# A fused attention-and-MoE kernel: TensorE work in a hand-written order, one MoE wave around each attention group, phi(q) on eight 32x64 tiles, and the denominator inverted once per token

## The chip, the cores and the metric

The kernel runs on one core of one Trainium2 chip. The metric is device time in microseconds (us), the median of several executions. A run more than 1.5% above the fastest of the same kernel is called slow, and ratios use fast runs alone.

Names: PE is TensorE, PEld its weight loads, DVE VectorE, ACT ScalarE, POOL GpSimd, SP the queue that issues most DMAs. PSUM is the memory that TensorE writes. "L220" in a profile line is line 220 of that kernel's text, so one product has different line numbers in different kernels.

## The reference

```python
# q, k, v: (4 batches, 4 heads, 1088 tokens, 32); S1, S2: (8, 32)
def phi(x):                                   # 64 features
    a, b = S1 @ x, S2 @ x                     # 8 each, per token
    return outer(a, b).reshape(64)
kv  = sum over tokens of phi(k) v^T           # 64 x 32 per head
z   = sum over tokens of phi(k)
num = phi(q) @ kv
den = phi(q) @ z + 1e-6
x   = (num / den), heads side by side         # 4352 tokens x 128
h   = x @ w_in                                # 128 -> 2048
g   = h * sigmoid(beta * h)
out = g @ w_out                               # 2048 -> 128
```

All inputs and the output are f32. The attention part is computed in f32, the two large products of the MoE in f16.

## The kernel before

x is kept turned (128 features on partitions, tokens along the row). beta is folded into the weights, so that g becomes a plain Silu. The MoE is cut into chunks of 512 tokens. A *wave* is two of the sixteen 128-wide slices of d_ff for one chunk: two products into two PSUM banks, one Silu of 128x1024 on ACT, then two products into the output bank (68 waves in all).

```python
    def wave():
        # ... (cut)
        for jj in range(jn):
            nc.tensor.matmul(out=wv[:, jj * tw : (jj + 1) * tw],
                             lhsT=winp[:, (j0 + jj) * P : (j0 + jj + 1) * P],
                             rhs=xT[:, t0 : t0 + tw], start=True, stop=True)
        nc.scalar.activation(out=g, in_=wv, func=ACTF.Silu)
        flush_w2()                            # second products of the wave before
        # ... (cut)
```

Attention of a batch is a generator of steps; behind each step up to two waves are emitted, if their tokens are ready. The framework's scheduler then orders each engine. phi(q) has two heads in one block-diagonal weight of 128 columns, on the 64 rows of these heads:

```python
        for c0, cw in q_chk:                  # 384, 384, 320 tokens
            for pi in range(2):
                rows = slice(64 * pi, 64 * pi + 64)
                nc.tensor.matmul(out=aps[:, :cw], lhsT=sa[rows, :],
                                 rhs=qT[rows, c0 : c0 + cw], start=True, stop=True)
                nc.scalar.copy(out=asb[pi][:, :cw], in_=aps[:, :cw])
            # ... (cut: bps with sb in the same way, then qp = bps * asb on DVE)
```

The denominator comes out of its product repeated for the 32 features of each head, and the whole of it is inverted:

```python
            for which, dst in ((1, den), (0, num)):
                for pi in range(2):
                    nc.tensor.matmul(out=dst[64 * pi : 64 * pi + 64, :cw],
                                     lhsT=nd[:, which, 64 * pi : 64 * pi + 64],
                                     rhs=qp[:, pi, c0 : c0 + cw], start=True, stop=True)
            nc.scalar.activation(out=deps[:, :cw], in_=den[:, :cw], func=ACTF.Identity, bias=epsb)
            nc.vector.reciprocal(out=deps[:, :cw], in_=deps[:, :cw])       # 128 x 384
            nc.vector.tensor_tensor(out=xT[:, ...], in0=num[:, :cw], in1=deps[:, :cw], op=MUL)

    for b in range(B):
        steps = attention(b)
        # ... (cut: weights prepared in batch 0)
        for _ in steps:
            pump(2)                           # two waves behind each step
    pump(10**6)
```

## Time and profile before

| what | value | view |
|---|---|---|
| time | 181.4 us | median of 3 runs |
| span | 180.2 us | page |
| busy PE, ACT, DVE | 82%, 49%, 45% | page, part 1 |
| first MoE wave | 41.1 us | timeline |
| period of a batch (den to den) | 37.1, 37.7, 34.7 us | chain of waits |
| tail, two waves | 2.19 us | timeline of ACT |

Two lines of the page of the kernel before: PE's busy time with its count of instructions, and the TensorE clock that was granted, in tenths, in 40 equal slices of the span.

```profile
PE 147.1 (82%) x1201; PEld 59.9 (33%) x1201; DVE 82.0 (45%) x113; ACT 88.9 (49%) x122; POOL 15.0 (8%) x17
...
PEclk9999999699999999969999999999999995799998
```

PE is the bound, but the MoE streams only 2 x 69,632 columns, and in the chain two matmuls of 512 take 0.43 us, so it needs about 58 us of the 147. The rest is attention, switching and slow clock. The chain of waits of the kernel before, inside a batch (start, length, what):

```profile
85.86 0.43 PE wave L220 x2
86.29 0.84 PE aps L293 x2
87.13 0.54 PE moeout L180 x2
87.67 0.43 PE wave L220 x2
...
90.34 0.85 PE bps L301 x4
91.19 0.54 PE wave L220 x2
```

A lone aps product (two records, as every f32 product here) takes 0.84 us; two bps products on the two row halves take 0.85 together. A pair of MoE matmuls takes 0.43, and 0.54 when it follows an attention group. Next the groups of instructions of the kernel before: line, engine, operation, out<-in, shapes, count, busy us, mean ns.

```profile
L359 DVE RECIPROCAL deps<-deps 128x384 f32<-128x384 f32 (+1 forms) x12 | 28.4, 2395 | 7.0 <-ACT deps L358 7.0
...
L293 PE MATMUL aps<-qT,sa 64*128 64x384 f32 (+1 forms) x48 | 22.0, 581 | 0.1
...
L301 PE MATMUL bps<-qT,sb 64*128 64x384 f32 (+1 forms) x48 | 16.5, 544 | 0.0
```

And the end of attention in a batch, from the timeline of the kernel before (start, length, engine, what; in brackets the idle time before it and what ended it):

```profile
71.24 4.96 DVE L359 RECIPROCAL deps<-deps 128x384 f32<-128x384 f32 x2 [1.98 <-ACT deps L358]
...
76.12 0.96 DVE L360 TENSOR_TENSOR xT<-num,deps 128x384 f16<-128x384 f32 x2
...
76.67 1.33 PE L350 MATMUL num<-qp,nd 128*64 128x320 f32 x2 [3.15 <-DVE xT L360]
77.94 1.89 PE L220 MATMUL wave<-xT,winp 128*128 128x512 f16 x4
```

DVE inverts for 5 us, PE stands for 3.15, and then four wave matmuls take 1.89 us instead of 0.87: the clock has been halved (the 6 in slice 18 of the clock row; 0.58 granted in the mean from 76 to 80 us).

### The profile page before, as it was taken

To read this page: it belongs to the slowest core of one execution; us is meant where nothing else is said; L and a number is where in the kernel's file an instruction comes from. 1 tells how busy PE (TensorE), PEld (TensorE's weight loads), DVE (VectorE), ACT (ScalarE), POOL (GpSimd) and SP (SyncE) were. 2 spreads that over 40 slices of the span, in tenths; PEclk is the share of its full clock that TensorE was granted. 3 is DMA by queue.
4 is the path that set the end of the run, shared out by engine and by line. 5 is a ranking of instruction groups with operands and counts; after the bars stand their busy time and mean duration, and the time that the engine had idled before them with its cause. 6 is when DMAs were issued, how large, how long until landed. Compare 5 with 4: busy or idle time off the path is not lost.

```text
span 180.2 us, 2944 instructions
## 1 busy us (share of the span) xinstructions
PE 147.1 (82%) x1201; PEld 59.9 (33%) x1201; DVE 82.0 (45%) x113; ACT 88.9 (49%) x122; POOL 15.0 (8%) x17
## 2 busy tenths in 40 slices
PE   0079996849999998399999977999999738988870
PEld 0023555312333363023333632333336202333350
DVE  1268374798725322977032128954222496101010
ACT  0230132119666745054966452869664215588870
POOL 2006340000320000000500000005000000000000
PEclk9999999699999999969999999999999995799998
DMA  5699999300003000030003000300300300002131
GB/s 182 169 382 340 318 249 254 93 4 2 0 0 58 5 4 0 0 58 0 0 7 55 4 0 0 58 4 0 58 0 4 52 6 4 0 0 41 19 60 29
DMA packets 22480, 11.35 MB, mean 63 GB/s; under 512 B 18738, under 2 KB 20802, under 8 KB 22338
## 3 DMA queue, kind: packets, MB, share of 16 engines
q1 hardware_dynamic: 22304, 11.15, 25.1%
q8 instruction: 9, 0.15, 0.3%
q10 hardware_dynamic: 162, 0.02, 0.1%
q14 instruction: 5, 0.03, 0.1%
HBM read 8.94 MB, written 2.23 MB: 62 GB/s over the span
## 4 chain that ended last, share of the span: by engine, by line
PE 68%; ACT 9%; DVE 9%; issue 7%; DMA 4%; ACTq 0%; SPq 0%; DVEq 0%
PE wave L220 17%; PE moeout L180 16%; PE aps L293 10%; ACT g L228 7%; PE kvz L314 6%; PE bps L301 5%; PE kps L261 5%; DVE deps L359 4%; PE bb L152 4%; PE num L350 3%; DMA v<-in_v_dram 3%; PE den L350 2%; DMA sraw<-in_S_dram 1%; ACT deps L358 1%; DVE xT L360 1%
## 5 line engine op out<-in xcount | busy, mean ns | idle before, releaser
L228 ACT ACTIVATE g<-wave 128x1024 f16<-128x1024 f32 x68 | 66.2, 1021 | 28.9 <-PE wave L220 28.7
L220 PE MATMUL wave<-xT,winp 128*128 128x512 f16 (+1 forms) x144 | 42.7, 387 | 5.0 <-DVE xT L360 4.4
L180 PE MATMUL moeout<-g,woutp 128*128 128x512 f16 (+1 forms) x144 | 41.9, 375 | 4.0 <-ACT g L228 4.0
L359 DVE RECIPROCAL deps<-deps 128x384 f32<-128x384 f32 (+1 forms) x12 | 28.4, 2395 | 7.0 <-ACT deps L358 7.0
L304 DVE TENSOR_TENSOR qp<-bps,asb 128x384 f32<-128x384 f32 (+1 forms) x24 | 12.4, 533 | 30.2 <-PE bps L301 30.0
L293 PE MATMUL aps<-qT,sa 64*128 64x384 f32 (+1 forms) x48 | 22.0, 581 | 0.1
L220 PEld LDWEIGHTS <-winp 128*128 128x128 f16 x144 | 13.2, 100 | 26.2 <-issue 15.5
L180 PEld LDWEIGHTS <-woutp 128*128 128x128 f16 x144 | 12.1, 98 | 26.7 <-issue 17.7
L297 ACT COPY asb<-aps 128x384 f32<-128x384 f32 (+1 forms) x24 | 11.2, 465 | 17.6 <-PE aps L293 12.8
L358 ACT ACTIVATE deps<-den,epsb 128x384 f32<-128x384 f32 (+1 forms) x12 | 6.7, 562 | 25.2 <-DVE xT L360 13.8
L277 POOL TENSOR_TENSOR kp<-kab 128x576 f32<-128x576 f32 x8 | 10.2, 1291 | 105.8 <-DVE kab L268 105.8
L350 PE MATMUL num<-qp,nd 128*64 128x384 f32 (+1 forms) x48 | 13.8, 535 | 5.7 <-DVE xT L360 5.7
L261 PE MATMUL kps<-kT,sw 32*32 32x288 f32 x128 | 9.4, 480 | 10.2 <-DVE sw L119 9.6
L301 PE MATMUL bps<-qT,sb 64*128 64x384 f32 (+1 forms) x48 | 16.5, 544 | 0.0
L190 DVE STREAM_TRANSPOSE o_sb<-moeout 128x512 f32<-128x512 f32 (+1 forms) x9 | 6.1, 676 | 19.1 <-PE moeout L180 19.0
L350 PE MATMUL den<-qp,nd 128*64 128x384 f32 (+1 forms) x48 | 10.7, 525 | 1.3 <-DVE nd L343 1.2
L293 PEld LDWEIGHTS aps<-qT,sa 64*128 64x128 f32 x48 | 7.9, 205 | 9.9 <-issue 8.0
L268 DVE STREAM_TRANSPOSE kab<-kps 128x288 f32<-128x288 f32 x16 | 7.2, 466 | 7.1 <-PE kps L261 7.1
L314 PE MATMUL kvz<-kp,ones 128*32 128x64 f32 (+1 forms) x288 | 9.5, 219 | 0.0
L314 PE MATMUL kvz<-kp,v 128*32 128x64 f32 (+1 forms) x288 | 9.3, 222 | 0.0
L301 PEld LDWEIGHTS bps<-qT,sb 64*128 64x128 f32 x48 | 7.4, 205 | 3.9 <-issue 1.3
L350 PEld LDWEIGHTS num<-qp,nd 128*64 128x64 f32 x48 | 4.2, 153 | 13.2 <-DVE xT L360 6.8
(43 smaller groups left out, 75.1 us busy)
## 6 DMA issues: line engine op xcount, KB each, us to landing
v<-in_v_dram SPq DMA_DIRECT2D x16, 144.0 KB, 8.4
k<-in_k_dram SPq DMA_DIRECT2D x4, 544.0 KB, 4.6
q<-in_q_dram SPq DMA_DIRECT2D x4, 544.0 KB
out_dram<-o_sb SPq DMA_DIRECT2D x20, 64.0 KB, 2.0
w_in_sb<-in_moe_w_in_dram SPq DMA_DIRECT2D x1, 1024.0 KB
out_dram<-o_sb SPq DMA_DIRECT2D x4, 56.0 KB, 1.9
out_dram<-o_sb SPq DMA_DIRECT2D x4, 48.0 KB
out_dram<-o_sb SPq DMA_DIRECT2D x4, 40.0 KB, 1.7
```

What stands on the lines that cost most here:

```text
L180: nc.tensor.matmul(out=moe["acc"][:, :tw], lhsT=woutp[:, j, :], rhs=g[:, jj, :tw], start=(j == 0), stop=(j == NJ - 1),)
L220: nc.tensor.matmul(out=wv[:, jj * tw : (jj + 1) * tw], lhsT=winp[:, (j0 + jj) * P : (j0 + jj + 1) * P], rhs=xT[:, t0 : t0 + tw], start=Tru ...
L228: nc.scalar.activation(out=g, in_=wv, func=ACTF.Silu)
L261: nc.tensor.matmul(out=kps[32 * g : 32 * g + 32, : NJK * 32], lhsT=sw[rows, :], rhs=kT[rows, KBASE[g] * 32 : (KBASE[g] + NJK) * 32], start ...
L277: eng.tensor_tensor(out=kp[:, h].rearrange("p j (i l) -> p j i l", i=R), in0=bass.AP(tensor=a0.tensor, offset=a0.offset, ap=[pst, [32, NJK ...
L293: nc.tensor.matmul(out=aps[:, :cw], lhsT=sa[rows, :], rhs=qT[rows, c0 : c0 + cw], start=True, stop=True)
L297: nc.scalar.copy(out=asb[pi][:, :cw], in_=aps[:, :cw])
L301: nc.tensor.matmul(out=bps[:, :cw], lhsT=sb[rows, :], rhs=qT[rows, c0 : c0 + cw], start=True, stop=True)
L304: nc.vector.tensor_tensor(out=qp[:, pi, c0 : c0 + cw], in0=bps[:, :cw], in1=asb[pi][:, :cw], op=MUL)
L314: nc.tensor.matmul(out=kvz[32 * h : 32 * h + 32, F * which : F * which + F], lhsT=v_t[b][:kr, h, j, :] if which == 0 else ones[:kr, :], rh ...
L350: nc.tensor.matmul(out=dst[64 * pi : 64 * pi + 64, :cw], lhsT=nd[:, which, 64 * pi : 64 * pi + 64], rhs=qp[:, pi, c0 : c0 + cw], start=Tru ...
L359: nc.vector.reciprocal(out=deps[:, :cw], in_=deps[:, :cw])
```

## The change

The intent: shorten what attention costs TensorE, shorten the way from den to x, and lay attention groups and waves in a fixed alternation so that ACT and PE always have work. Five parts:

1. **Order.** Each batch is 15 groups; a slot emits the first products of a wave, one group, then the second products of the wave before. TensorE's instructions are taken in the order of the text (`manual_schedule`).
2. **phi(q) on 32x64 tiles:** one head's 32 rows, 64 features, for one half of the tokens; up to eight such products at once. Token blocks of 32 alternate between the two halves of the partitions. num goes to 64x32 tiles, kps to 64x32.
3. **Denominator turned:** den has two useful rows per head (one for each half). DVE transposes 32x32 blocks, adds epsilon, inverts 18 columns, and transposes a broadcast of it back.
4. **Start:** two small loads of S1 and S2 instead of eight, q of batch 0 on ACT's queue, half of the broadcast of beta before anything else, the weights scaled on POOL.
5. PSUM is redivided: a product's PSUM tile has one or two banks, and `aps` shares the two buffers of the waves.

```diff
+    ctx.enter_context(tc.manual_schedule(engines={mybir.EngineType.PE}))
 ...
+    def slot(group=None):
+        if moe["ci"] < len(tok_chk) and sum(tok_chk[moe["ci"]]) <= moe["ready"]:
+            w1()
+        if group is not None:
+            group()
+        ...
+        while len(todo) > 1:
+            w2(*todo.pop(0))
 ...
+                for c in range(2):
+                    for m in range(2):
+                        for pr, n, dst, sx in mm:          # aps of one pair of heads, bps of the other
+                            h = 2 * pr + m
+                            rows = slice(32 * h, 32 * h + 32)
+                            nc.tensor.matmul(
+                                out=dst[64 * c : 64 * c + 64, m, : 32 * tn],
+                                lhsT=sx[rows, :],
+                                rhs=qT[rows, t0 : t0 + tn, c, :], ...)
 ...
-            nc.scalar.activation(out=deps[:, :cw], in_=den[:, :cw], func=ACTF.Identity, bias=epsb)
-            nc.vector.reciprocal(out=deps[:, :cw], in_=deps[:, :cw])
+                nc.vector.transpose(out=dT[...], in_=dps[:, :w])
+                nc.vector.tensor_scalar_add(rc[:, :tn], dT[:, :tn, :2], 1e-6)
+                nc.vector.reciprocal(out=rc[:, :tn], in_=rc[:, :tn])
+                nc.vector.transpose(out=rb[...], in_=<rc, each value 32 times>)
 ...
+        return [kps, ab((0, 0), None), ab((1, 0), (0, 0)), kv([1, 2]), ab((0, 1), (1, 0)),
+                kv([3, 4]), ab((1, 1), (0, 1)), kv([5, 6]), ab(None, (1, 1)), kv([7, 8, 0]),
+                ndt, den(0), num(0), den(1), num(1)]
 ...
-        for _ in steps:
-            pump(2)
+        for n, grp in enumerate(groups):
+            slot(grp)
+        slot()
+        slot()
```

## The prediction

> **What bounds the kernel now.** The span is 180.2 us. The page's first part has PE busy 82%, ACT 49%, DVE 45%; the chain of waits gives PE 68%, so TensorE is the bound, but much of it is not streaming. The two MoE products stream 2 x 69,632 columns; in the chain two back-to-back 512-column matmuls take 0.43 us, so the MoE needs about 58. Four things are lost around that (timeline, windows, chain):
>
> 1. Before the first MoE wave, at 41.1 us, only attention of batch 0 runs: sketch weights wait for eight small loads until 9.6, the broadcast of beta takes 7.2, the denominator section holds 32.7 to 41.1.
> 2. phi(q) (aps, bps): 22.0 and 16.5 us busy. A lone 64x128 product of 384 columns takes 0.84 us; two fit the array.
> 3. Every switch between MoE and attention products costs: a MoE pair takes 0.54 instead of 0.43 after one, and a group's last product drains about 0.2. The scheduler switches per product.
> 4. Denominator: reciprocal on 128x384 takes 2.53 us; all twelve, 28.4 us DVE. From den to the first xT a batch takes 5 to 7 us with PE mostly waiting, and the clock falls: 0.76 granted in 142 to 156, where four wave matmuls take 1.86 instead of 0.87.
>
> One batch's period (den to den) is 37.1, 37.7, 34.7 us.
>
> **What the change does.** The Trainium skill ("TensorEngine Tiling (Array Packing)", Available Configurations) lists 32x64 as eight tiles. The trace agrees that such small tiles run together: 11 kps products of 288 columns end within 0.74 us. So a full phi(q) group (four aps, four bps products, 288 or 256 columns) should take 0.6 to 0.7, five groups a batch 3.3, against about 7 now. den and num fall from 3.6 to about 2.2, kps to one group of 0.65. kvz keeps 2.2 but is cut in four groups (+0.8). Attention becomes about 10 us of PE per batch, MoE with one switch per slot 15.5.
> The reciprocal handles 18 columns (about 0.25, as rbeta's 16), plus two DVE transposes (288: 0.47; 576: about 0.75) and an add: 1.7 per chunk instead of 2.6 + ACT. ACT per batch: 16 waves x 1.08 + 4 asb copies x 0.65 + 0.4 = 20; DVE about 15. Neither binds overall, but in phi(q) slots ACT (1.02 + 0.65) matches PE (1.75).
>
> **Sum.** A slot with wave and group: 1.75 us. Per batch: 14 such, one num slot without a wave and with a bubble waiting for DVE (2.0), two wave-only slots bound by ACT (1.1 each): 28.7.
> Start: sketch weights earlier, half the beta broadcast before k lands, weights prepared on POOL; first wave near 27. Rest of batch 0: 5.5. Three batches: 86. Tail, 16 waves at the 1.095 of now: 17.5. Last product, transpose, output DMA: 5.5; launch 1.2. Sum 142.7; I add 3 for in-order stalls. **Predicted 146 us, range 138 to 158; faster 0.97, same 0.02, slower 0.01.**
>
> **What would show it.** First wave at 25 to 30 us. Period 27 to 31. aps+bps PE under half. DVE total under 75. Granted clock near 1.00 from the first wave on. Chain: PE and ACT, with DVE only at num. Tail rate unchanged.
>
> **What would make it wrong.** PE in hand order stops at any late operand: qT or kp late behind other DVE/POOL work, the single "two" bank pair, or aps sharing buffers with the waves (copy and Silu in one loop), giving 2.1 us slots and 158. Eight tiles not overlapping would add about 2 us per batch. Weights late from POOL would move the first wave past 30.

## The result

The changed kernel takes 142.9 us (141.7 to 143.7, 4 runs) against 181.6 us. The ratio is 0.786, with a 95% interval of 0.779 to 0.793. Ratios here are the mean time of one kernel's fast runs over that of the other's fast runs of the same rounds, so they are not quite the ratio of the medians.

The same lines of the page of the changed kernel:

```profile
PE 118.4 (84%) x1393; PEld 46.9 (33%) x1393; DVE 61.9 (44%) x111; ACT 83.8 (60%) x98; POOL 22.7 (16%) x24
...
PEclk9999998557999999999999999999999999999998
```

29 us of PE time and 20 us of DVE time are gone. The clock is halved for a while near 24 to 33 us and full after that. The chain of waits of the changed kernel, inside a batch:

```profile
68.25 0.54 PE moeout L197 x2
68.78 0.54 PE wave L233 x2
69.32 0.58 PE kvz L361 x32
69.91 0.54 PE moeout L197 x2
70.44 0.43 PE wave L233 x2
70.88 0.35 PE aps L328
```

A slot is a pair of `wave`, a group, and a pair of `moeout`: 1.66 us here, from the wave at 68.78 to the one at 70.44. The 14 slots of this batch with a wave and a group take 22.2 us together, 1.59 each; the slot of `ndt` takes 1.08, and that of the last kv 1.92. (The wave at 68.78 follows no group; its 0.54 holds a wait of 0.1 us for ACT, whose Silu ends at 68.68.) The group of phi(q) on the page of the changed kernel:

```profile
L328 PE MATMUL aps<-qT,s_151 32*64 32x288 f32 (+1 forms) x128 | 12.9, 454 | 0.2
```

And its reciprocals, in the groups with shapes kept apart:

```profile
L420 DVE RECIPROCAL rc<-rc 128x18 f32<-128x18 f32 x4 | 1.1, 266 | 0.1
L420 DVE RECIPROCAL rc<-rc 128x16 f32<-128x16 f32 x4 | 1.0, 253 | 0.1
```

The reciprocal has fallen from 28.4 us to 2.1. The end of attention in a batch, from the timeline of the changed kernel:

```profile
82.73 0.48 DVE L417 STREAM_TRANSPOSE dT<-dps 128x288 f32<-128x288 f32 x1 [0.90 <-PE dps L408]
...
83.75 0.78 DVE L424 STREAM_TRANSPOSE rb<-rc 128x576 f32<-128x576 f32 x1
84.63 0.76 DVE L450 TENSOR_TENSOR xT<-nps,rb 128x576 f16<-128x576 f32 x1
85.44 0.59 PE L233 MATMUL wave<-xT,winp 128*128 128x512 f16 x2 [1.59 <-DVE xT L450]
```

From the end of den to x it is now 2.7 us, PE stands for 1.59, and the clock holds.

Where the time went, stage by stage in the two profiles (us; the tail is counted from the last sixteen waves on):

| stage | before | after |
|---|---|---|
| start to the first wave | 41.1 | 30.3 |
| first wave to the tail | 115.7 | 86.0 |
| tail to the end | 23.4 | 24.2 |

So 30 us of the gain lie between the first wave and the tail, about 10 for each of the three later batches (period 26.7 instead of 34.7 to 37.7), and 11 lie in the start. The tail gained nothing; it is 0.8 us longer.

### The profile page after: what moved, and what is told of

Same layout as the page of the kernel before. It is cut to its first block, busy times and chain, and to the rows that moved or that the text cites. A ratio compares the mean times of both kernels' runs of the same rounds, so it can differ in the third digit from the quotient of the medians.

```text
span 140.5 us, 3293 instructions
## 1 busy us (share of the span) xinstructions
PE 118.4 (84%) x1393; PEld 46.9 (33%) x1393; DVE 61.9 (44%) x111; ACT 83.8 (60%) x98; POOL 22.7 (16%) x24
## 3 DMA queue, kind: packets, MB, share of 16 engines
q1 hardware_dynamic: 22160, 10.59, 30.3%
## 4 chain that ended last, share of the span: by engine, by line
PE 59%; DMA 9%; DVE 9%; ACT 8%; SPq 6%; issue 4%; ACTq 0%; DVEq 0%
PE moeout L197 19%; PE wave L233 19%; ACT g L241 8%; PE kvz L361 6%; PE aps L328 5%; DMA q<-in_q_dram 5%; PE dps L408 4%; SPq L76 4%; DMA v<-in_v_dram 3%; PE bps L328 2%; DVE rb L424 2%; DVE xT L450 2%; PE nps L442 2%; DVE dT L417 1%; PE kps L280 1%
## 5 line engine op out<-in xcount | busy, mean ns | idle before, releaser
L233 PE MATMUL wave<-xT,winp 128*128 128x512 f16 (+1 forms) x144 | 41.1, 373 | 6.4 <-DVE xT L450 6.4
L343 DVE TENSOR_TENSOR qp<-bps,asb 128x576 f32<-128x576 f32 (+1 forms) x16 | 11.5, 719 | 23.7 <-PE bps L328 23.7
L328 PE MATMUL bps<-qT,s_153 32*64 32x288 f32 (+1 forms) x128 | 12.0, 436 | 2.3 <-DVE qp L343 2.3
L328 PE MATMUL aps<-qT,s_151 32*64 32x288 f32 (+1 forms) x128 | 12.9, 454 | 0.2
L338 ACT COPY asb<-aps 128x576 f32<-128x576 f32 (+1 forms) x16 | 9.7, 608 | 3.3 <-PE bps L328 3.1
L154 PE MATMUL bb<-beta_row,ones_row 1*128 1x512 f32 x8 | 7.5, 1092 | 3.3 <-DMA beta_row<-in_moe_beta_dram 3.3
L361 PEld LDWEIGHTS kvz<-kp,v 128*32 128x32 f32 (+1 forms) x288 | 6.7, 111 | 8.5 <-issue 6.3
L297 DVE TENSOR_TENSOR kp<-kab 128x576 f32<-128x576 f32 x8 | 9.5, 1224 | 0.0
L361 PEld LDWEIGHTS kvz<-kp,ones 128*32 128x32 f32 (+1 forms) x288 | 7.3, 114 | 0.0
L269 DVE STREAM_TRANSPOSE kT<-k 128x1088 f32<-128x1088 f32 x4 | 5.2, 1303 | 4.2 <-DMA k<-in_k_dram 4.2
L450 DVE TENSOR_TENSOR xT<-nps,rb 128x576 f16<-128x576 f32 (+1 forms) x8 | 5.8, 725 | 0.8
```

What stands on the lines that cost most here:

```text
L154: nc.tensor.matmul(out=bb[:, c], lhsT=ones_row, rhs=beta_row[:, o + 512 * c : o + 512 * c + 512], start=True, stop=True,)
L233: nc.tensor.matmul(out=wv[:, jj * tw : (jj + 1) * tw], lhsT=winp[:, (j0 + jj) * P : (j0 + jj + 1) * P], rhs=xT[:, t0 : t0 + tw], start=Tru ...
L297: eng.tensor_tensor(out=kp[:, h].rearrange("p j (i l) -> p j i l", i=R), in0=bass.AP(tensor=a0.tensor, offset=a0.offset, ap=[pst, [32, NJK ...
L328: nc.tensor.matmul(out=dst[64 * c : 64 * c + 64, m, : 32 * tn], lhsT=sx[rows, :], rhs=qT[rows, t0 : t0 + tn, c, :], start=True, stop=True,)
L338: nc.scalar.copy(out=asb[:, :, :w], in_=aps[:, :, :w])
L343: nc.vector.tensor_tensor(out=qp[:, 2 * pb : 2 * pb + 2, 32 * t0 : 32 * t0 + w], in0=bps[:, :, :w], in1=st[b_of][:, :, :w], op=MUL,)
```

## The experiments

The theory in the prediction: four things were lost (start, phi(q), switching by the scheduler, denominator), and the change takes back part of each. The first rival: one part carries all, and another may be worthless, the hand order above all. So each part was undone, as far as it could be alone.

### 1. TensorE's order given back to the scheduler (e1_auto)

```diff
-    ctx.enter_context(tc.manual_schedule(engines={mybir.EngineType.PE}))
```

> The changed kernel with the hand order of TensorE taken away: the framework's scheduler orders TensorE as it does in the kernel before. Theory (order matters: [...]the scheduler switches per product): 150 to 155 us, batch period 29 to 31 instead of 26.7. Rival (tiles and the cheap denominator carry the gain, order is worth little): under 146 us.

Measured: 139.8 us median (138.4 to 142.0); mean of its three fast runs 139.3, against 142.8 and 143.3 for the changed kernel. They were run at other times. The theory fell: taking the hand order away does not cost 8 us, it gains 3. The profile (of its slowest run, 142.0) shows nearly the same order in the batches. The scheduler kept the order of the text, with one exception that counts: it moved den of the second chunk (`dps`, 256 columns) up, into the time in which PE waits for x, as its timeline shows at the end of batch 2:

```profile
85.19 0.64 PE L407 MATMUL dps<-qp,zb 128*32 128x256 f32 x8
...
86.85 1.02 PE L232 MATMUL wave<-xT,winp 128*128 128x512 f16 x4 [0.48 <-DVE xT L449]
```

From den to den the later batches take 25.9 us each instead of 26.7. Batch 0 was no better in this profile: PE stood once for 4.45 us, and the first wave came at 32.8 us.

### 2. The order of the text undone (e5_pump)

```diff
-    ctx.enter_context(tc.manual_schedule(engines={mybir.EngineType.PE}))
-        for n, grp in enumerate(groups):
-            slot(grp)
+        for part in ((0,), (), (1, 2), (4, 6), (8,), (3, 5, 7, 9, 10), (11, 12), (13, 14)):
+            for n in part:
+                groups[n]()
+            slot()
+            slot()
```

> The changed kernel with the order of the old program: attention in eight steps (kps; all phi(q); kv whole with ndt; den and num by chunk), two waves behind each step, TensorE ordered by the framework's scheduler. With the run that gave TensorE back to the scheduler but kept the slots (139.8 us) it tells the order of the text from the flag. Theory (the slots of the text are what counts, the flag is not): 3 to 5 us more per batch, 149 to 156 us. Rival (the scheduler makes the same interleaving of any text): 139 to 143 us.

Measured: 149.7 us median (146.6 to 150.9). Only the run of 146.6 counts as fast, so the size is loose: at least 7 us above e1_auto (139.3). The granted clock of the four runs was 0.96 to 1.00, so the clock does not explain it. Busy time by engine over batches 1 and 2, first of e1_auto and then of e5_pump (stretch, its length, then PE, PEld, DVE, ACT, POOL; both profiles are of runs called slow, and in both the first stretch begins behind the first product of kps, which the scheduler had moved up):

```profile
39.43:65.59 26.16, 25.17 (x344) 9.73 (x351) 14.84 (x25) 18.23 (x21) 3.25 (x2) 1.00 0.14 23
65.59:91.47 25.88, 25.20 (x346) 9.73 (x353) 12.40 (x23) 18.32 (x22) 3.16 (x2) 1.00 0.14 22
```

```profile
38.83:67.38 28.55, 26.46 (x344) 10.79 (x351) 14.94 (x25) 17.78 (x21) 3.25 (x2) 1.00 0.13 20
67.38:96.16 28.78, 26.68 (x347) 10.88 (x353) 12.49 (x23) 18.39 (x22) 3.16 (x2) 1.00 0.13 20
```

The same 344 to 347 matmul records of a batch take 28.7 us instead of 26.0: about half of the difference is PE busy longer (the scheduler takes groups apart: at 40.80 us one bps product stands alone, for 0.69 us, where four together take 0.71 in the changed kernel), half is PE idle (2.1 us instead of 0.7 to 1.0). So the alternation of wave and group is worth something; the flag that fixes it is not what makes it so.

### 3. The old denominator in the changed kernel (e2_oldden)

```diff
-                nc.vector.transpose(out=dT[...], in_=dps[:, :w])
-                ... add, reciprocal of 18 columns, transpose
+                nc.scalar.activation(out=rb[:, :, :w], in_=dps[:, :, :w], func=ACTF.Identity, bias=epsb)
+                nc.vector.reciprocal(out=rb[:, :, :w], in_=rb[:, :, :w])
```

> The changed kernel with the old denominator: z in all 32 columns of each head, ACT adds epsilon, DVE takes the reciprocal of 128x576 (8 of these at about 6.6 ns per column, 3.8 us each, 29 us of DVE in all). Theory (the chain den to xT is exposed in every batch): about 2.5 us more per batch, 152 to 156 us, TensorE idle before the first wave of a batch 4 us instead of 1.6, clock low there. Rival (DVE has over half its time free, so it hides): under 146 us.

Measured: 161.7 us, 19 us more than the changed kernel where 9 to 13 were expected: the direction was right, the size was not. The first wave came at 34.1 us, and the period rose to 31.9 and 32.6. The timeline of this run at the end of batch 2 shows why it is so much:

```profile
93.47 3.75 DVE L419 RECIPROCAL rb<-rb 128x576 f32<-128x576 f32 x1 [2.19 <-ACT rb L416]
97.33 0.76 DVE L440 TENSOR_TENSOR xT<-nps,rb 128x576 f16<-128x576 f32 x1
98.14 1.01 PE L235 MATMUL wave<-xT,winp 128*128 128x512 f16 x2 [3.93 <-DVE xT L440]
```

PE stands for 3.93 us instead of 1.59, as expected; but after that its pair of wave matmuls takes 1.01 us and not 0.59. The clock is halved in the pause (0.50 granted from 98 to 102 us), and what follows runs at half speed for some us. I had named the low clock, but counted only the pause (the clock is 0.90 over this run, 0.96 in the changed kernel). The edit did one thing more: den now takes the one two-bank buffer that num uses too, so num waits for ACT to empty it, 2.8 us in all. The 19 us include what that costs, which was not measured apart.

### 4. The new denominator in the kernel before (b2_newden)

```diff
-            nc.scalar.activation(out=deps[:, :cw], in_=den[:, :cw], func=ACTF.Identity, bias=epsb)
-            nc.vector.reciprocal(out=deps[:, :cw], in_=deps[:, :cw])
+            (den on four 128x32 tiles; transpose, add, reciprocal of 12 columns, transpose)
```

> The kernel before, only with the turned denominator (z in one column of a 128x32 weight per head, transpose, epsilon and reciprocal of 12 columns, transposed back), its order and its phi(q) kept. Theory (the run with the old denominator in the changed kernel lost 19 us): 10 to 16 us less than before, 166 to 172 us, DVE busy 82 to about 62. Rival (the changed kernel is sensitive to the denominator only because the rest is fast): 174 us or more.

Measured: 170.9 us, ratio 0.944 to the kernel before (interval 0.933 to 0.955), 10.1 us less. DVE busy fell from 82.0 to 70.2, not to 62: I had left out the twenty-four transposes, 13 us. The granted clock of the profiled run rose from 0.96 to 0.99. So this part alone is worth 10 in the old order and 19 in the new one. Why it is worth less there was not tested; the first wave did not come earlier (41.7 us), so batch 0 gained nothing from it.

### 5. phi(q) back on two tiles (e3_oldphi)

```diff
-                                out=dst[64 * c : 64 * c + 64, m, : 32 * tn],
-                                lhsT=sx[rows, :],                 # 32 rows, 64 columns
+                            out=dst[:, pi, :cw],
+                            lhsT=sx[rows, :],                 # 64 rows, 128 columns, block-diagonal
```

Order, start and the turned denominator were kept; num went back to 128x64 and there were three chunks of tokens.

> The changed kernel with phi(q) back on two 64x128 tiles (three chunks of 384, 384, 320), num on 128x64, den on 128x32, hand order and turned denominator kept. Theory (TensorE time in the slots is the bound): 3 to 4 us more per batch, 154 to 160 us, TensorE busy up by 10 or more. Rival (slots are bound by ACT and waits, not by these products): under 147 us.

Measured: 149.6 us, 6.6 us more (fast mean 149.4). Per batch the expectation held: the period was 29.7 and 30.6 us, 3 to 4 more, and PE busy rose by 9. The total missed it because batch 0 lost nothing: the first wave came at 30.1 us as in the changed kernel, and the clock was 1.00 in the whole profile. Slower products in a stage that waits anyway cost nothing here. Why the clock held was not tested: PE was busy for only 1.26 of the 4 us from 26 to 30 us in this profile, and the profile of e5_pump keeps 1.00 as well, with the short products.

### 6. The old start (e4_oldstart)

```diff
-    nc.scalar.dma_start(out=sraw[:R, :], in_=S1)            # and S2
+    for g in range(4):  # S1 and S2 four times each
-    beta_bcast(0)                                           # ahead of all
+                    beta_bcast(0); beta_bcast(1)            # behind kps; w_in scaled on DVE, w_out in one POOL operation
```

> The changed kernel with the old start: eight sketch loads, q of batch 0 behind v on the sync queue, the whole broadcast of beta after kps, w_in scaled on DVE and w_out in one POOL operation. Theory: first wave 4 to 6 us later (kps 2.5 later, half a broadcast of 3.8 more before phi(q)), 146 to 149 us, period unchanged. Rival (the stall at 18 to 21 us, where DVE waits for q of batch 1, absorbs it): 142 to 144 us.

Measured: 152.2 us, 9.3 more, first wave at 39.2 us, periods unchanged (26.8 and 26.7). That is more than I expected, and the reason is in the hand order: the broadcast of beta stood at 12.2 to 24.1 us on PE, because its PSUM buffers were freed by DVE only behind its work on k and q, and PE in fixed order could not go around it. In the kernel before the same broadcast took 7.2 us. So this run does not measure the old start alone: its 9.3 us include that blocking, and what the new start is worth without it stays open.

### 7. The waits in batch 0 (c_after, m3_q1, m4_warm)

In the first profile of the changed kernel PE stands at 19 to 21.5 us, because DVE, which works in order, has the two transposes of batch 1 (kT and qT, 1.3 us each, with a wait of 0.51 us for q of batch 1 between them) ahead of a product of batch 0; after that the clock is halved. First a control on the same chip as m3_q1:

> Control: the changed kernel once more, so that the runs of this call have it on the same chip. 142 to 144 us, period 26.7 us.

Measured: 143.1 us (142.8 to 144.3).

m3_q1 loads q of batch 1 earlier:

```diff
     q_t[0] = load_rows(nc.scalar, q, 0, "q")
+    q_t[1] = load_rows(nc.scalar, q, 1, "q")
```

> The changed kernel, only with the load of q of batch 1 issued right behind q of batch 0 on the ACT queue. Theory: the 2.3 us for which TensorE stood at 19 to 21.5 us (DVE, in order, waiting for that load before the product that TensorE needed) goes, and with it most of the half clock from 22 to 33 us: first wave 3 to 4.5 us earlier, 138 to 140 us. Rival (the DMA queues are full then, so another load comes later instead): no gain, 142 us or more.

Measured: 142.7 us, 0.7 less by fast means: close to nothing. The first wave came at 28.7 us, 1.6 earlier. The wait of PE for DVE (in all, times, longest), first of the changed kernel, then of the control, then of m3_q1:

```profile
PE bps L328 <- DVE qp L343: 2.3, 1, 2.3
...
PE bps L328 <- DVE qp L343: 0.8, 1, 0.8
...
PE bps L330 <- DVE qp L345: 0.6, 1, 0.6
```

So the long wait was already gone in the control, where DVE did not wait for q of batch 1 at all: m3_q1 tested a wait that comes and goes from run to run. And without it the clock fell all the same, in the control (0.50 from 26 to 34 us, first wave at 30.3) and in m3_q1 (0.50 from 28 to 34), and first waves and den ran in it. The expectation that the clock would follow was wrong.

m4_warm keeps the waits and puts work of no use into them:

```diff
+            if b == 0 and n in WARM:       # {8: 5, 10: 1, 11: 2, 13: 5}
+                warm(WARM[n])              # matmuls 128x256 f32 into the unused output bank
```

> The changed kernel, only with 13 matmuls of no use (128x256 f32, into the bank that no one uses yet) put where TensorE stands in batch 0. Theory: the half clock from 22 to 34 us comes from these pauses and costs 2 to 3 us; the clock stays at 1.00, the first waves take 0.43 a pair instead of 0.97, 140 to 141 us. Rival (the useless work stands in the way as long as it saves, or the clock does not care): 143 us or more.

Measured: 141.1 us (140.7 to 142.0), a mean 2.1 us below the control and 1.6 below the changed kernel's first runs. It was run at another time. The profiled runs, 142.0 and 142.3 us, differ by 0.3 only. So the effect on the clock is shown, and its worth, 0.3 to 2.1 us, is not settled. Busy time and clock by stretch (PE first after the length; the clock is the third number from the right), first of the changed kernel and then of m4_warm:

```profile
24.00:26.00 2.00, 0.94 (x10) 0.30 (x4) 0.45 (x3) 1.66 (x2) 0.00 (x0) 0.50 1.08 251
28.00:30.00 2.00, 0.64 (x16) 0.10 (x1) 1.79 (x5) 0.00 (x0) 0.00 (x0) 0.50 1.08 266
32.00:34.00 2.00, 2.00 (x23) 0.47 (x20) 1.64 (x3) 1.04 (x2) 0.00 (x0) 0.64 0.04 13
```

```profile
24.00:26.00 2.00, 1.61 (x27) 1.17 (x28) 0.00 (x0) 0.86 (x2) 0.00 (x0) 1.00 1.12 203
28.00:30.00 2.00, 2.00 (x17) 1.65 (x10) 1.90 (x5) 0.00 (x0) 0.00 (x0) 1.00 1.03 301
32.00:34.00 2.00, 2.00 (x29) 0.52 (x23) 1.83 (x5) 1.92 (x2) 0.00 (x0) 1.00 0.28 74
```

The clock stays at 1.00 throughout. The first wave comes 1.0 us later (31.3 instead of 30.3 us), and the first kps of batch 1 still comes slightly earlier (36.7 instead of 37.0): what follows the pause has caught up.

### 8. The wait for x in each batch (m2_hold)

```diff
-            slot(grp)
+            slot(grp, wave=not (b > 0 and n in HOLD))       # HOLD = (2, 6)
+            if b > 0 and n == 12:
+                slot()
```

> The changed kernel, only with two waves of each later batch held back from the slots of the 2nd and 4th phi(q) group and put around and behind the first num. Theory: TensorE's 1.6 us wait for DVE (transpose, reciprocal, transpose, product) before the first wave of each new chunk is exposed and is filled: period 25.0 to 25.5 instead of 26.7, 138 to 139 us. Rival (the wait overlaps with what ACT needs anyway): period above 26.3, 142 us.

Measured: 140.3 us (fast mean 140.1 against 143.3 of the control on the same chip). The theory held in kind: the wait for x is gone in three of four batches (6.4 us before, 1.6 left). The period fell to 26.2 and 25.8 us, less than expected, because part of the wait returned elsewhere: with a slot shortened, kv comes so early that PE waits for POOL's product kp, 2.2 us in all, a wait that the changed kernel does not have.

### 9. The repairs together (best1, best2)

best1 has the useless matmuls in batch 0 and q of batch 1 early. Two waves are held back, den of the second chunk has a held wave in its slot ahead of the new chunk's first, and in the tail two waves are pending instead of one:

```diff
-        slot()
+        slot(depth=2)                      # tail: w2 of a wave only after w1 of the next two
```

> The changed kernel with four repairs: two waves held back and den of the 2nd chunk moved up into the wait for DVE, q of batch 1 early, useless matmuls in the pauses of batch 0, and in the tail two waves pending instead of one, so that ACT does not wait. Expected: period 25 to 25.8, tail pair of waves 2.06 instead of 2.195, clock 1.00: 134 to 137 us.

> The same with TensorE left to the framework's scheduler, slots kept. If the flag itself costs (139.8 against 143 us without repairs): 1 to 3 us less than best1. If the gain there was only that den of the 2nd chunk is moved up, which best1 has too: within 1 us of best1.

Measured: 136.2 us for each (135.3 to 136.4, and 135.2 to 136.4), ratios 0.750 and 0.751 to the kernel before. Both are faster than both kernels. As the second case of the expectation had it, the scheduler gains nothing once den is moved up by hand. That fits the move having been its gain in e1_auto; no run made the move alone. Of the 5.9 us between the profiled spans (140.5 and 134.6), batch 0 gave 2.0, batches 1 and 2 gave 1.1 and the rest 2.8. The period (26.3 us from kps of batch 2 to that of batch 3) did not reach 25 to 25.8; PE waits for POOL's kp here too (2.6 us in all). The tail gained more than I expected. ACT in the tail of the changed kernel, and then of best1 (start, length, count at the end):

```profile
119.01 1.94 ACT L241 ACTIVATE g<-wave 128x1024 f16<-128x1024 f32 x2 [0.26 <-PE wave L233]
121.21 1.94 ACT L241 ACTIVATE g<-wave 128x1024 f16<-128x1024 f32 x2 [0.26 <-PE wave L233]
```

```profile
113.26 8.36 ACT L243 ACTIVATE g<-wave 128x1024 f16<-128x1024 f32 x9 [0.26 <-PE wave L235]
```

Two Silus every 2.20 us became nine in 8.36, so 0.93 each. In the order w1, w2 of the wave before, w1, every second Silu waits for PE, and PE waits for ACT; one more wave pending breaks that loop. The Trainium skill's page "ScalarE: Activation LUTs", section What ACT_TABLE_LOAD costs, gives 186 ns + 0.833 ns per element for one ACTIVATE with immediates, 1.04 us for 1024 (an estimate from the page), and says that such instructions overlap by about 93 ns when they follow each other directly; the trace agrees, with 1.02 us for one and 0.93 in the row of nine. The tail was also in the kernel before at 2.19, and the change left it so.

### What the parts are worth

| part undone in the changed kernel | cost, us |
|---|---|
| turned denominator | 19.1 |
| start (with PE blocked by the broadcast) | 9.3 |
| 32x64 tiles for phi(q), with num and chunks | 6.6 |
| order of the text (against e1_auto, one fast run) | 7.2 |
| fixing that order by the flag | -3.5 |

The costs are differences of the means of fast runs. Each row compares runs of different calls; the changed kernel itself took 142.8 in one and 143.3 in another, so half a us is open in each. They add up to 38.7, near the gain of 38.9, but they are not independent (the denominator alone is worth 10.1 in the kernel before), so the closeness of the sum is partly luck.

## Why the prediction was right

**The size.** The sum was 142.7 us and the measured median 142.9. The sum was closer than its terms. The first wave was expected at 27 and came at 30.3; the rest of batch 0 was expected at 5.5 and took 6.8; the three batches were expected at 86 and took 79; tail and end were expected at 23.0 and took 24.2; the launch was expected at 1.2, and the profiled run was 1.8 longer than its span. Errors of about plus 6 and minus 7 us cancelled. The 3 us that I added for stalls of an order fixed by hand were not needed on top; the predicted 146 is that much too high, and well inside its range.

**What bounds the kernel.** Right: PE, in batches 1 and 2 busy for 25.1 of 26.7 to 27.1 us in the changed kernel; I had estimated 10 + 15.5. The Trainium skill's page "TensorEngine Tiling (Array Packing)", section Available Configurations, lists eight 32x64 tiles; the trace agrees: the 16 records of a full phi(q) group start within 0.34 us of each other and end 0.74 us after the first start. My figure of 0.6 to 0.7 us per group held nearly.

**A slot.** Expected 1.75 us, measured 1.59 in the mean of a batch's 14 slots. This is the term that was mis-sized in the batches: 0.16 us in each of 14 slots in three batches make 6.7 of the 7 us. ACT, which I took as equal to PE in phi(q) slots, was busy for 18.5 us per batch, not 20.

**The denominator.** Right in mechanism: I expected one num slot per batch with an exposed wait for DVE, 2.0 us in all; it takes 2.3 (num, and then the wait of 1.59). The prediction had also named the slow clock behind the old pause (0.76 granted); the expectation of e2_oldden left it out of the sum, and was too low.

**The order.** Here the step "The scheduler switches per product" failed as an explanation. The scheduler follows the order of the text as nearly as it can: with the text's slots and no flag it gives the same alternation and is 3 us faster (e1_auto), and with the old text it loses at least 7 (e5_pump). The switching cost itself is as I read it (0.54 against 0.43 for a pair after a group, in both kernels). The same skill page, section Key Properties, says that a change of tiling mode drains the array; the 0.11 us agree with it, and so does `ndps`: behind that f32 group on the full 128x128 array (0.22 us at 80.93) the pair takes 0.43, so it is not the change from f32 to f16 that costs.

**The start.** The direction was right, the mechanism incomplete: PE's waits in batch 0 and the half clock behind them were not foreseen.

**The signs named beforehand.** First wave at 25 to 30: 30.3, just outside. Period 27 to 31 (den to den): 28.9 from batch 0 on, then 26.7 twice, just outside on the good side. aps and bps busy under half: wrong as written, 24.9 of 38.5 us, because the busy time of a line counts tiles of one group that run together with those of the other line. DVE under 75: 61.9. Clock near 1.00 from the first wave on: wrong, 0.50 until about 33. Chain PE and ACT, with DVE only at num: right after the first wave, but for 0.30 us at `nd` in batch 1. Tail unchanged: right.

## What to carry to other kernels

Before fixing an engine's order by hand, write the program text in the wanted order and leave the scheduler free: the text gave the gain, and the freedom gave 3 us more by filling a wait. Price a pause of TensorE at its length plus the slow clock that may follow it; in a stage that must wait, a few matmuls of no use can be cheaper than the pause. A wait that is filled can come back at the next late operand (here POOL's kp), so look for it before counting the gain.

## What the Trainium skill lacked or had wrong

- "TensorE: Matmul & The Clock Gate", Part 1 and its practical table, ties the half clock to an idle window of about 3.4 us and asks for no gap over about 3 us. Here the clock fell in batch 0 with no single wait of PE over 2.34 us ahead of it, from 8 us on: 0.50 from about 24 to 33 us in the changed kernel, where PE had been busy for 1.66 of the 4 us from 18 to 22. In the control c_after it fell soon after 24 us with no wait over 0.82 us from 8 us on, and PE busy for 2.66 of the 4 us from 20 to 24. So low busy time over some us can be enough. It need not be: in e3_oldphi the clock stayed at 1.00 with PE busy for 1.26 of the 4 us from 26 to 30. What decides between them no run here shows. (The same Part does tell of a kernel in which frequent short idles made the clock go up and down, without a figure for them.) That the page's gate is activity-driven agrees with m4_warm (1.00 throughout).
- "TensorEngine Tiling (Array Packing)", Key Properties, names the drain at a change of mode but gives no cost. Here a pair of f16 matmuls takes 0.54 us behind a group on small tiles against 0.43 behind another pair.
- No page gives a time for DVE's reciprocal; here it takes 2.53 us for 384 columns and 3.75 us for 576 (6.5 to 6.6 ns per column), 0.27 us for 18.
